# Gated attention and token MLP on one core: one transpose for the bias rows, and Wk loaded in two held halves

## The chip, the cores and the metric

The kernel runs on one core of one Trainium2 chip. The metric is device time in microseconds (us) of one execution. TensorE is called PE here, VectorE DVE, ScalarE ACT, GpSimd POOL and SyncE SP, as the profile calls them. SP, ACT and POOL each issue DMA transfers from a queue of their own.

## The reference

The input `x` has 2048 rows of 512 numbers in bfloat16. The output mixes two branches with a gate per row:

```
g   = sigmoid((x * gate_w).sum(-1))
qkv = x @ wqkv                      # 512 x 1536; 32 heads of 16
a   = attention(q, k, v) @ wo       # each row sees 8 earlier rows, 2 apart, softmax over them
h   = layernorm(x)
u   = gelu(h.T @ w1 + b1)           # token MLP: 2048 -> 1792
b   = (u @ w2 + b2).T               # 1792 -> 2048
out = g * a + (1 - g) * b
```

`b1` has 1792 numbers, `b2` has 2048 and `gate_w` has 512. On the chip they are needed as columns, with 128 of them down the partitions: 14 columns for `b1`, 16 for `b2`, 4 for `gate_w`.

## The kernel before

The kernel is a list of operations, each with an engine, an estimated duration, the named results that it reads and writes, and a priority. A list scheduler at build time (`_Sched`) puts them into one fixed order per engine and works out the semaphore waits. All PE operations are chained, so PE runs them in the order in which they are written. On each of the DMA queues the loads of the beginning are chained in the same way.

The beginning, which the change is about, goes like this.

- POOL fills `ONES`, makes the identity `IDENT` from it (L458 to L461), and then issues three small loads: `gate_w` into `GWR` (4 rows of 128), `b1` into `B1R` (14 rows) and `b2` into `B2R` (16 rows) (L523 to L525). All three lie side by side in a region `ROWS`, each from partition 0 on. After that POOL writes padding and mask.
- SP and ACT issue the first loads in turn (L517 to L521): 128-row tiles 0 and 2 of `x` and quarters 0 and 2 of Wq on SP, tiles 1 and 3 and quarters 1 and 3 on ACT. Each has 128 KB. Then SP goes on alone, in this order: Wk as one load of 512 KB (L522), Wv (512 KB), and three times four tiles of `x` (512 KB) followed by a transposing load of the same rows into `XT`, and the first part of `w1`.
- PE starts with matmuls on constants that need no data (`f_warm`, L546). Then it transposes tiles 0 and 1 of `x` (`f_tx`, L562), DVE and ACT copy the results to `XT`, and PE multiplies with Wq, quarter by quarter of the contraction (`f_q0`, L583): `q0_0_0` and `q0_0_1`, with 256 columns. It transposes tiles 2 and 3, and does four more of these groups (16 matmuls of 256 columns).
- Next PE turns the bias rows into columns with three small transposes (`f_tb`, L599 to L601), into bank 7 of PSUM; DVE copies them out (L612 to L614). Then comes the last quarter of Wq over all 512 columns (`q0_2_3`).
- Then the projections run, 512 columns and four matmuls per PSUM bank each (`f_proj`, L650): K of the first 512 rows (four banks, "K block 0"), V of the first 512 rows (four banks), and then the rest, which reads the transposed loads. ACT empties the banks. A ring of seven banks is used in turn.

From there PE works through the projections (L650), the first layer of the MLP (L848), its second layer (L875) and the output product (L884). DVE does the attention in long element-wise operations (L449) beside it. PE takes their sums at L707 and L712 and their result at L884.

Of the kernel before, what the change touches and what calls it, by code (L numbers as in the profile page):

```python
# [5 lines left out]
BF16 = mybir.dt.bfloat16  # L6
# [7 lines left out]
D = 512  # L14
# [4 lines left out]
NST = S // 128  # L19
NFT = F // 128  # L20
# [260 lines left out]
class _Mem:  # L281
# [17 lines left out]
    def view(self, name, dtype, dims, extra=0, p0=0, np_=128):  # L299
        base = self.arena[:].bitcast(dtype)  # L300
        pst = base.ap[0][0]
        esz = mybir.dt.size(dtype)
        o = self.off[name]
        assert o % esz == 0
        return bass.AP(base.tensor, p0 * pst + o // esz + extra, [[pst, np_]] + [list(d) for d in dims])


def bass_gated_mix__sliding_local_dilated__mixer_token_mlp__prompt_kernel(nc, A_x, A_wqkv, A_wo, B_x, B_w1, B_b1, B_w2, B_b2, gate_w, out, dbg=None):
    with contextlib.ExitStack() as es:
        block = es.enter_context(nc.Block())  # L310
        m = _Mem(nc, es)
# [23 lines left out]
        m.region("OUTS", 5 * D * 2)  # L335
        m.region("RP", 32 * 2)
        m.region("GWREP", 4 * 32 * 2)
        m.region("ROWS", 384 * 2)
        m.region("MASK", NW * PAD * 2)
        m.region("SMALL", 2048)  # L340
        m.alias("UT", "WQKV")
# [4 lines left out]
        view = m.view  # L346
# [3 lines left out]
        A = sch.add  # L350
# [3 lines left out]
        wqkv_v = A_wqkv.rearrange("(dt p) c -> p dt c", p=128)  # L354
# [7 lines left out]
        WQKV = view("WQKV", BF16, [(3 * D, 4), (1, 3 * D)])  # L362
# [37 lines left out]
        IDENT = view("IDENT", BF16, [(1, 128)])  # L400
        ONES = view("ONES", BF16, [(1, 128)])
        RP = view("RP", BF16, [(1, 32)])
        GWREP = view("GWREP", BF16, [(32, 4), (1, 32)])
        MASK = view("MASK", BF16, [(PAD, NW), (1, PAD)], np_=32)
        B1R = view("ROWS", BF16, [(1, 128)], np_=NFT)
        B2R = view("ROWS", BF16, [(1, 128)], extra=128, np_=NST)
        GWR = view("ROWS", BF16, [(1, 128)], extra=256, np_=4)
        so = [0]

        def small(n, dims=None, extra=0):  # L410
# [21 lines left out]
        B2C = small(NST)  # L432
# [5 lines left out]
        def psb(bank):  # L438
            return ps[:, bank, :].bitcast(BF16)

        def sub(ap_, offs, dims):
            return bass.AP(ap_.tensor, ap_.offset + offs, [list(ap_.ap[0])] + [list(d) for d in dims])
# [12 lines left out]
        GELU = "gelu_apprx_tanh_and_others"  # L455
# [6 lines left out]
        A("pool", lambda e: e.memset(sub(KH[0], 0, [(KR, 4), (1, PAD)]), 0.0), 0.2, writes=["kpad"], name="kpad")  # L462
        A("pool", lambda e: e.memset(sub(V5, 0, [(VR, 4), (1, PAD)]), 0.0), 0.2, writes=["vpad"], name="vpad")

        def f_mask(e):
            ins = None
            for w in range(NW):
                if w:
                    ins = e.memset(psub(MASK, 0, 32, w * PAD, [(1, 2 * w)]), NEG)
                if 2 * w < PAD:  # L470
                    ins = e.memset(psub(MASK, 0, 32, w * PAD + 2 * w, [(1, PAD - 2 * w)]), 0.0)
            return ins
# [12 lines left out]
        def load(name, dst, src, nbytes, writes, transpose=False, queue="sp", issue=0.5, order=True, deps=(), after=()):  # L485
            ds = sch.dsem(name)

            def fn(e):
                if transpose:
                    return e.dma_start_transpose(dst, src)  # L490
                return e.dma_start(dst, src)  # L491
            op = sch.dma(queue, fn, nbytes, ds, issue=issue, writes=writes, deps=list(deps) + late_dep[0],
                         after=list(after) + ([last_ld[queue]] if order and queue in last_ld else []), name=name)
            if order:
                last_ld[queue] = op
            return op
# [14 lines left out]
        def xq(t, queue):  # L511
            return ld_first("x%d" % t, X[:, t:t + 1, :], xv[:, t:t + 1, :], 131072, ["x%d" % t], queue)

        def wqq(k_, queue):
            return ld_first("wq%d" % k_, WQKV[:, k_:k_ + 1, 0:D], wqkv_v[:, k_:k_ + 1, 0:D], 131072, ["wq%d" % k_], queue)

        for k_ in (0, 2):  # L517
            xq(k_, "sp")
            xq(k_ + 1, "act")
            wqq(k_, "sp")  # L520
            wqq(k_ + 1, "act")  # L521
        load("wk", WQKV[:, 0:4, D:2 * D], wqkv_v[:, 0:4, D:2 * D], 4 * 128 * D * 2, ["wk"])  # L522
        load("gw", GWR, gate_w.rearrange("(t p) -> t p", p=128), 1024, ["gwr"], issue=0.6, queue="pool")  # L523
        load("b1", B1R, B_b1.rearrange("(t p) -> t p", p=128), 4096, ["b1r"], issue=0.6, queue="pool")
        load("b2", B2R, B_b2.rearrange("(t p) -> t p", p=128), 4096, ["b2r"], issue=0.6, queue="pool")  # L525
        ld_w("wv", 2, 0, 4, "wv")
        for k_ in range(1, 4):
            ld_x(4 * k_, 4)
# [22 lines left out]
        def PE(fn, dur, reads, writes, name, prio=0):  # L551
            op = A("pe", fn, dur, reads=reads, writes=writes, after=([chain[0]] if chain[0] is not None else []), name=name, prio=prio)
            chain[0] = op
            return op
# [41 lines left out]
               "q0_%d_%d" % (hb, dt))  # L596

        def f_tb(e):
            e.transpose(out=psb(7)[:, 512:512 + NFT], in_=B1R, identity=IDENT[0:NFT, 0:NFT])  # L599
            e.transpose(out=psb(7)[:, 576:580], in_=GWR, identity=IDENT[0:4, 0:4])  # L600
            return e.transpose(out=psb(7)[:, 544:544 + NST], in_=B2R, identity=IDENT[0:NST, 0:NST])  # L601

        pe_tx(0)
        pe_q0(0, 0)
# [3 lines left out]
        pe_q0(1, 0)  # L608
        pe_q0(1, 1)
        pe_q0(1, 2)  # L610
        PE(f_tb, 0.17, ["b1r", "b2r", "gwr", "ident"], ["b7"], "t_b12")
        A("dve", lambda e: e.tensor_copy(out=GWREP, in_=sub(psb(7), 576, [(1, 4), (0, 32)])), 0.2, reads=["b7"], writes=["gwrep"], name="gwrep", prio=-20)  # L612
        A("dve", lambda e: e.tensor_copy(out=B1C, in_=psb(7)[:, 512:512 + NFT]), 0.15, reads=["b7"], writes=["b1c"], name="b1c", prio=-20)
        A("dve", lambda e: e.tensor_copy(out=B2C, in_=psb(7)[:, 544:544 + NST]), 0.15, reads=["b7"], writes=["b2c"], name="b2c", prio=-20)  # L614
        pe_q0(2, 3)
        XT0 = ["xt0_%d_%d" % (t, k_) for t in range(4) for k_ in range(2)]

# [3 lines left out]
        def evac(tn, dl, sb, bank, eng="act"):  # L621
            h, o = sb // 2, (sb % 2) * 512
            if tn == 0:
                dst = QH[h][:, dl, o:o + 512]
                A(eng, act(dst, ps[:, bank, :], AF.Copy, scale=0.25) if eng == "act" else
                  (lambda e: e.tensor_scalar(out=dst, in0=ps[:, bank, :], scalar1=0.25, scalar2=None, op0=ALU.mult)), 0.6,
                  reads=["b%d" % bank], writes=["q%d_%d" % (dl, sb)], name="evq%d_%d" % (dl, sb), prio=0 if eng == "act" else -25)
            elif tn == 1:
                dst = KH[h][:, dl, PAD + o:PAD + o + 512]
                A("act", act(dst, ps[:, bank, :], AF.Copy), 0.6, reads=["b%d" % bank], writes=["k%d_%d" % (dl, sb)],  # L630
                  name="evk%d_%d" % (dl, sb))
            else:
                dst = V5[:, dl, PAD + sb * 512:PAD + (sb + 1) * 512]
                A("act", act(dst, ps[:, bank, :], AF.Copy), 0.6, reads=["b%d" % bank], writes=["v%d_%d" % (dl, sb)],
                  name="evv%d_%d" % (dl, sb))
# [5 lines left out]
        def bank_():  # L641
            b = ring[1][ring[0] % len(ring[1])]
            ring[0] += 1
            return b

        def f_proj(tn, dl, sb, bank):
            def fn(e):
                ins = None
                for dt in range(4):
                    ins = e.matmul(ps[:, bank, :], lhsT=sub(WQKV, dt * 3 * D + tn * D + dl, [(4, 128)]),  # L650
                                   rhs=XT[:, dt, sb * 512:(sb + 1) * 512], start=(dt == 0), stop=(dt == 3))
                return ins
            return fn

        WR = {0: ["wq0", "wq1", "wq2", "wq3"], 1: ["wk"], 2: ["wv"]}

        def proj(tn, dl, sb):
            bank = bank_()
            PE(f_proj(tn, dl, sb, bank), 0.87, xt_res(sb) + WR[tn], ["b%d" % bank], "pj%s%d_%d" % ("qkv"[tn], dl, sb))
            evac(tn, dl, sb, bank)  # L660

        for dl in range(4):
            proj(1, dl, 0)
        for dl in range(4):
            proj(2, dl, 0)
        for dl in range(4):
# [3 lines left out]
          reads=["k%d_1" % dl for dl in range(4)], writes=["khalo"], name="khalo")  # L670
# [10 lines left out]
        for t in range(NST):  # L681
            A("dve", (lambda t_: lambda e: e.bn_stats(out=ST6[:, t_, :], in_=X[:, t_, :]))(t), 0.67,  # L682
              reads=["x%d" % t], writes=["st%d" % t], name="st%d" % t, prio=-20, after=[extl["dve"]])
# [6 lines left out]
          reads=["md"], writes=["vv"], name="ln_var", prio=-20)  # L690
# [3 lines left out]
          reads=["ms", "rstd"], writes=["nmr"], name="ln_nmr", prio=-20)  # L694
# [159 lines left out]
        for ft in range(NFT):  # L854
            bank = MLPB[ft]
            for half in range(2):
                PE(f_ph2(ft, bank, half), 1.735, ["x%d" % t for t in range(8 * half, 8 * half + 8)] + [W1R[ft // 2]], ["b%d" % bank],
                   "ph2_%d_%d" % (ft, half))
            A("act", act(UT[:, ft, :], ps[:, bank, :], AF.Gelu_apprx_tanh, bias=col(B1C, ft)), 0.7,
              reads=["b%d" % bank, "b1c"], writes=["ut%d" % ft] + (["wq0", "wq1", "wq2", "wq3", "wk", "wv"] if ft == 0 else []), name="gel%d" % ft, table=GELU)  # L860
            if ft % 2 == 1 and ft // 2 + 5 <= 6:
                ld_w1(ft // 2 + 5)
        for j in range(8):
# [40 lines left out]
        for i, half in head + tuple((i, half) for i in range(3, L) for half in range(2)):  # L904
            bank = banks[i]
# [103 lines left out]
```

## Time and profile before

| | |
|---|---|
| median of 5 runs | 166.07 us (165.59 to 166.25) |
| the profiled execution | 167.1 us, of which 165.4 us are the span from the first to the last instruction |
| granted PE clock over the span | 1.000 |
| PE | busy 160.4 us, 97% of the span |
| DVE | busy 150.8 us, 91% |
| ACT | busy 75.5 us, 46% |
| POOL | busy 13.7 us, 8% |

The profile is one execution. The timeline view gives the start and the duration of an instruction, or of a row of equal ones, from the span's start. Matmuls overlap in the pipeline: each is recorded for longer than the distance to the next, so the distance between starts is the time that one takes from PE. "Idle before" is the time that an engine waited, and what released it. For DMA, the view of issues gives the time from the start of the issue to the landing of the last byte. Rows marked SPq and ACTq are those queues' issue work.

### The profile page before, as it was taken

What the parts mean: (1) busy time and instruction counts of PE and PEld (TensorE: products, weight loads), DVE (VectorE), ACT (ScalarE), POOL (GpSimd) and SP (SyncE); (2) the same over time, 40 slices, a digit from 0 to 9 for tenths busy, and PEclk for the clock granted to TensorE, in tenths of its full rate; (3) what the DMA queues carried; (4) which work ended last, traced back from release to release, by engine and by line L of the source; (5) the groups of instructions that cost most, each with busy time, mean ns of one, the idle gap of its engine ahead of it and who ended that gap; (6) DMA issues with size and microseconds to landing.
All of it is one profiled execution on the core that took longest, in us unless ns stands there. A gap on an engine that the chain in (4) does not pass through costs nothing.

```text
span 165.4 us, 1993 instructions
## 1 busy us (share of the span) xinstructions
PE 160.4 (97%) x795; PEld 78.2 (47%) x810; DVE 150.8 (91%) x126; ACT 75.5 (46%) x104; POOL 13.7 (8%) x38
## 2 busy tenths in 40 slices
PE   7899999999999999999999999999999999999993
PEld 3665555555544444444444344444444444444551
DVE  0389999999999999999999999999999999999940
ACT  3327678667765399962221559310022111111164
POOL 7000110020000000005000000005000222000000
PEclk9999999999999999999999999999999999999999
DMA  5999989509399096999998983993995899981014
GB/s 141 300 289 270 226 187 256 115 15 190 63 292 317 26 244 180 298 290 285 168 220 231 271 244 101 302 271 108 284 231 170 163 207 189 210 187 35 32 54 137
DMA packets 44696, 32.24 MB, mean 195 GB/s; under 512 B 7952, under 2 KB 42256, under 8 KB 44688
## 3 DMA queue, kind: packets, MB, share of 16 engines
q1 hardware_dynamic: 41360, 22.06, 50.5%
q0 software_dynamic: 2608, 9.45, 28.3%
q10 hardware_dynamic: 720, 0.62, 1.1%
q8 instruction: 6, 0.10, 0.2%
q14 instruction: 2, 0.02, 0.0%
HBM read 18.88 MB, written 2.10 MB: 127 GB/s over the span
## 4 chain that ended last, share of the span: by engine, by line
PE 94%; DMA 2%; ACT 1%; issue 1%; SPq 0%
PE ps L848 29%; PE ps L875 29%; PE ps L650 23%; PE ps L884 8%; PE ps L583 3%; DMA arena<-in_A_wqkv_dram 2%; PE ps L712 1%; ACT arena L452 1%; PE ps L707 1%; PE ps L562 1%; SPq L491 0%; PE ps L599 0%; PE ps L601 0%; PE ps L600 0%
## 5 line engine op out<-in xcount | busy, mean ns | idle before, releaser
L449 DVE TENSOR_TENSOR arena<-arena 128x4096 bf16<-128x4096 bf16 (+8 forms) x79 | 132.1, 1719 | 1.4 <-ACT arena L452 0.3
L875 PE MATMUL ps<-arena 128*128 128x512 bf16 (+2 forms) x234 | 50.0, 366 | 0.2
L848 PE MATMUL ps<-arena 128*128 128x512 bf16 x218 | 48.5, 379 | 0.3
L452 ACT ACTIVATE arena<-ps,arena 128x512 bf16<-128x512 f32 (+1 forms) x30 | 21.8, 731 | 59.0 <-PE ps L884 41.0
L452 ACT ACTIVATE arena<-ps 128x512 bf16<-128x512 f32 (+3 forms) x53 | 33.1, 629 | 19.7 <-PE ps L650 10.6
L650 PE MATMUL ps<-arena 128*128 128x512 bf16 x173 | 38.0, 379 | 0.2
L875 PEld LDWEIGHTS ps<-arena 128*128 128x128 bf16 x238 | 22.8, 98 | 25.9
L848 PEld LDWEIGHTS ps<-arena 128*128 128x128 bf16 x224 | 21.7, 98 | 26.8 <-ACT arena L452 0.7
L650 PEld LDWEIGHTS ps<-arena 128*128 128x128 bf16 x176 | 19.9, 113 | 18.1
L884 PE MATMUL ps<-arena 128*128 128x512 bf16 (+2 forms) x67 | 15.6, 366 | 0.1
L944 ACT ACT_TABLE_LOAD x11 | 14.1, 1283 | 2.9 <-issue 2.7
L780 POOL DMA_DIRECT2D arena<-arena x8 | 4.4, 562 | 74.2 <-DVE arena L449 74.2
L884 PEld LDWEIGHTS ps<-arena 128*128 128x128 bf16 x68 | 6.5, 98 | 7.3
L682 DVE BATCH_NORM_STATS2 arena<-arena 128x6 f32<-128x512 bf16 x16 | 9.9, 678 | 0.0
L452 ACT ACTIVATE arena<-arena 128x16 f32<-128x16 f32 (+5 forms) x10 | 6.8, 679 | 6.2 <-DVE arena L449 6.0
L574 DVE COPY arena<-ps 128x256 bf16<-128x256 bf16 x4 | 1.2, 291 | 5.2 <-PE ps L562 4.9
L583 PE MATMUL ps<-arena 128*128 128x256 bf16 (+1 forms) x27 | 5.0, 348 | 0.7 <-DMA arena<-in_A_wqkv_dram 0.5
L696 DVE TENSOR_SCALAR arena<-arena 128x512 bf16<-128x512 bf16 x16 | 5.3, 407 | 0.0
L817 POOL DMA_DIRECT2D arena<-arena x3 | 3.6, 1200 | 19.0 <-DVE arena L449 19.0
L737 POOL DMA_DIRECT2D arena<-arena x2 | 2.5, 1234 | 30.0 <-DVE arena L449 30.0
L583 PEld LDWEIGHTS ps<-arena 128*128 128x128 bf16 x28 | 3.3, 128 | 1.7 <-DVE arena L574 0.8
L924 DVE TENSOR_SCALAR arena<-ps,arena 128x128 bf16<-128x128 f32 x1 | 0.4, 409 | 3.9 <-PE ps L884 3.9
(35 smaller groups left out, 19.8 us busy)
## 6 DMA issues: line engine op xcount, KB each, us to landing
arena<-in_B_w_dram SPq DMA_DIRECT2D x7, 1024.0 KB, 9.5
arena<-in_B_w_dram SPq DMA_DIRECT2D x8, 896.0 KB, 8.4
arena<-arena POOLq DMA_DIRECT2D x5, 1024.0 KB, 9.5
arena<-arena POOLq DMA_DIRECT2D x8, 512.0 KB, 11.0
out_dram<-arena SPq DMA_DIRECT2D x15, 128.0 KB, 1.7
arena<-in_A_x_dram SPq DMA_DIRECT2D x3, 512.0 KB, 4.8
arena<-in_A_wqkv_dram SPq DMA_DIRECT2D x2, 512.0 KB, 6.7
arena<-in_A_wo_dram SPq DMA_DIRECT2D x1, 512.0 KB, 8.8
```

The costliest lines, as they stand in the source:

```text
L449: return lambda e: e.tensor_tensor(out=o_, in0=a_, in1=b_, op=op_)
L452: return lambda e: e.activation(out=o_, in_=i_, func=f_, **kw)
L583: ins = e.matmul(ps[:, dl, c0:c1], lhsT=sub(WQKV, dt * 3 * D + dl, [(4, 128)]), rhs=XT[:, dt, c0:c1], start=(dt == 0 and hb == 0), stop=(d ...
L650: ins = e.matmul(ps[:, bank, :], lhsT=sub(WQKV, dt * 3 * D + tn * D + dl, [(4, 128)]), rhs=XT[:, dt, sb * 512:(sb + 1) * 512], start=(dt = ...
L682: A("dve", (lambda t_: lambda e: e.bn_stats(out=ST6[:, t_, :], in_=X[:, t_, :]))(t), 0.67, reads=["x%d" % t], writes=["st%d" % t], name="s ...
L696: A("dve", (lambda t_: lambda e: e.tensor_scalar(out=X[:, t_, :], in0=X[:, t_, :], scalar1=col(RSTD, t_), scalar2=col(NMR, t_), op0=ALU.mu ...
L780: prev = sch.dma("pool", (lambda d_, s_: lambda e: e.dma_start(d_, s_))(dst, src), 524288, sch.dsem("av%d_%d" % (h, c)), issue=1.0, reads= ...
L817: sch.dma("pool", (lambda o_, i_: lambda e: e.dma_start(o_, i_, accum_op=ALU.add, max_dma_last_dim=4096))(pw(0, 4), pw(4, 4)), 1800000, sc ...
L848: ins = e.matmul(ps[:, bank, :], lhsT=W1H[ft // 2][:, st, 128 * (ft % 2):128 * (ft % 2) + 128], rhs=X[:, st, :], start=(st == 0), stop=(st ...
L875: ins = e.matmul(ps[:, bank, 0:c1 - c0], lhsT=W2S[i // 2][:, ft, 128 * (i % 2):128 * (i % 2) + 128], rhs=UT[:, ft, c0:c1], start=(ft == 0) ...
L884: ins = e.matmul(ps[:, bank, 0:c1 - c0], lhsT=OT[:, i // 2, dl, 128 * (i % 2):128 * (i % 2) + 128], rhs=WO[:, dl, c0:c1], start=False, sto ...
L944: e.preload_act_table_set(want)
```

## The change

The three small loads go into one tile `ROWS` of 128 x 128, at partitions 0, 16 and 32. POOL writes zeros to all of the tile before. One 128 x 128 transpose replaces the three, and DVE picks the columns from other places. Wk is loaded in two halves of 256 KB (quarters 0 and 1 of the contraction, and 2 and 3). Both wait until tile 0 of `x` has landed; they stay at the same place of SP's queue, after the four first loads and ahead of Wv. The first two banks of K block 0 are filled in matching halves: two matmuls into the first bank, two into the second, then the other two of each. The other two banks go as before. A resource list at the first gelu names the two halves in place of the one load.

In the built programs the order of all other operations on every engine is the same in both. POOL has one memset more, ahead of that for `ONES`; SP has one issue more; PE has two matmuls less.

```diff
-        m.region("ROWS", 384 * 2)
+        m.region("ROWS", 128 * 2)
...
+        ROWS = view("ROWS", BF16, [(1, 128)])
         B1R = view("ROWS", BF16, [(1, 128)], np_=NFT)
-        B2R = view("ROWS", BF16, [(1, 128)], extra=128, np_=NST)
-        GWR = view("ROWS", BF16, [(1, 128)], extra=256, np_=4)
+        B2R = view("ROWS", BF16, [(1, 128)], p0=16, np_=NST)
+        GWR = view("ROWS", BF16, [(1, 128)], p0=32, np_=4)
...
+        rows0 = A("pool", lambda e: e.memset(ROWS, 0.0), 0.15, name="rows0", prio=-90)
...
+        xld = {}
         for k_ in (0, 2):
-            xq(k_, "sp")
+            xld[k_] = xq(k_, "sp")
...
-        load("wk", WQKV[:, 0:4, D:2 * D], wqkv_v[:, 0:4, D:2 * D], 4 * 128 * D * 2, ["wk"])
-        load("gw", GWR, ..., issue=0.6, queue="pool")
-        load("b1", B1R, ..., issue=0.6, queue="pool")
-        load("b2", B2R, ..., issue=0.6, queue="pool")
+        for k_ in range(2):
+            load("wk%d" % k_, WQKV[:, 2 * k_:2 * k_ + 2, D:2 * D], wqkv_v[:, 2 * k_:2 * k_ + 2, D:2 * D], 2 * 128 * D * 2, ["wk%d" % k_], deps=[xld[0]])
+        load("gw", GWR, ..., issue=0.6, queue="pool", deps=[rows0])
+        load("b1", B1R, ..., issue=0.6, queue="pool", deps=[rows0])
+        load("b2", B2R, ..., issue=0.6, queue="pool", deps=[rows0])
...
         def f_tb(e):
-            e.transpose(out=psb(7)[:, 512:512 + NFT], in_=B1R, identity=IDENT[0:NFT, 0:NFT])
-            e.transpose(out=psb(7)[:, 576:580], in_=GWR, identity=IDENT[0:4, 0:4])
-            return e.transpose(out=psb(7)[:, 544:544 + NST], in_=B2R, identity=IDENT[0:NST, 0:NST])
+            return e.transpose(out=psb(7)[:, 512:640], in_=ROWS, identity=IDENT)
...
-        PE(f_tb, 0.17, ["b1r", "b2r", "gwr", "ident"], ["b7"], "t_b12")
+        PE(f_tb, 0.06, ["b1r", "b2r", "gwr", "ident"], ["b7"], "t_b12")
...
-        for dl in range(4):
+        kb0 = [bank_() for dl in range(2)]
+        for k_ in range(2):
+            for dl in range(2):
+                PE(f_proj(1, dl, 0, kb0[dl], 2 * k_, 2 * k_ + 2), 0.44, XT0 + ["wk%d" % k_], ["b%d" % kb0[dl]], "pjk%d_0_%d" % (dl, k_))
+                if k_ == 1:
+                    evac(1, dl, 0, kb0[dl])
+        for dl in range(2, 4):
             proj(1, dl, 0)
```

More of the change, by code (lines that the diff above doesn't have):

```diff
@@ L521, in bass_gated_mix__sliding_local_dilated__mixer_token_mlp__prompt_kernel @@
             wqq(k_ + 1, "act")
-        load("wk", WQKV[:, 0:4, D:2 * D], wqkv_v[:, 0:4, D:2 * D], 4 * 128 * D * 2, ["wk"])
-        load("gw", GWR, gate_w.rearrange("(t p) -> t p", p=128), 1024, ["gwr"], issue=0.6, queue="pool")
-        load("b1", B1R, B_b1.rearrange("(t p) -> t p", p=128), 4096, ["b1r"], issue=0.6, queue="pool")
-        load("b2", B2R, B_b2.rearrange("(t p) -> t p", p=128), 4096, ["b2r"], issue=0.6, queue="pool")
+        for k_ in range(2):
+            load("wk%d" % k_, WQKV[:, 2 * k_:2 * k_ + 2, D:2 * D], wqkv_v[:, 2 * k_:2 * k_ + 2, D:2 * D], 2 * 128 * D * 2, ["wk%d" % k_], deps=[xld[0]])
+        load("gw", GWR, gate_w.rearrange("(t p) -> t p", p=128), 1024, ["gwr"], issue=0.6, queue="pool", deps=[rows0])
+        load("b1", B1R, B_b1.rearrange("(t p) -> t p", p=128), 4096, ["b1r"], issue=0.6, queue="pool", deps=[rows0])
+        load("b2", B2R, B_b2.rearrange("(t p) -> t p", p=128), 4096, ["b2r"], issue=0.6, queue="pool", deps=[rows0])
         ld_w("wv", 2, 0, 4, "wv")
@@ L610, in bass_gated_mix__sliding_local_dilated__mixer_token_mlp__prompt_kernel @@
         pe_q0(1, 2)
-        PE(f_tb, 0.17, ["b1r", "b2r", "gwr", "ident"], ["b7"], "t_b12")
-        A("dve", lambda e: e.tensor_copy(out=GWREP, in_=sub(psb(7), 576, [(1, 4), (0, 32)])), 0.2, reads=["b7"], writes=["gwrep"], name="gwrep", prio=-20)
+        PE(f_tb, 0.06, ["b1r", "b2r", "gwr", "ident"], ["b7"], "t_b12")
+        A("dve", lambda e: e.tensor_copy(out=GWREP, in_=sub(psb(7), 544, [(1, 4), (0, 32)])), 0.2, reads=["b7"], writes=["gwrep"], name="gwrep", prio=-20)
         A("dve", lambda e: e.tensor_copy(out=B1C, in_=psb(7)[:, 512:512 + NFT]), 0.15, reads=["b7"], writes=["b1c"], name="b1c", prio=-20)
-        A("dve", lambda e: e.tensor_copy(out=B2C, in_=psb(7)[:, 544:544 + NST]), 0.15, reads=["b7"], writes=["b2c"], name="b2c", prio=-20)
+        A("dve", lambda e: e.tensor_copy(out=B2C, in_=psb(7)[:, 528:528 + NST]), 0.15, reads=["b7"], writes=["b2c"], name="b2c", prio=-20)
         pe_q0(2, 3)
@@ L644, in bank_, with f_proj @@
             return b
-        def f_proj(tn, dl, sb, bank):
+        def f_proj(tn, dl, sb, bank, d0=0, d1=4):
             def fn(e):
                 ins = None
-                for dt in range(4):
+                for dt in range(d0, d1):
                     ins = e.matmul(ps[:, bank, :], lhsT=sub(WQKV, dt * 3 * D + tn * D + dl, [(4, 128)]),
@@ L653, in f_proj @@
             return fn
-        WR = {0: ["wq0", "wq1", "wq2", "wq3"], 1: ["wk"], 2: ["wv"]}
+        WR = {0: ["wq0", "wq1", "wq2", "wq3"], 1: ["wk0", "wk1"], 2: ["wv"]}
         def proj(tn, dl, sb):
@@ L859, in bass_gated_mix__sliding_local_dilated__mixer_token_mlp__prompt_kernel @@
             A("act", act(UT[:, ft, :], ps[:, bank, :], AF.Gelu_apprx_tanh, bias=col(B1C, ft)), 0.7,
-              reads=["b%d" % bank, "b1c"], writes=["ut%d" % ft] + (["wq0", "wq1", "wq2", "wq3", "wk", "wv"] if ft == 0 else []), name="gel%d" % ft, table=GELU)
+              reads=["b%d" % bank, "b1c"], writes=["ut%d" % ft] + (["wq0", "wq1", "wq2", "wq3", "wk0", "wk1", "wv"] if ft == 0 else []), name="gel%d" % ft, table=GELU)
             if ft % 2 == 1 and ft // 2 + 5 <= 6:
```

## The prediction

> **What bounds the kernel now.** I read the engine shares first, then the chain that ended last, then the timeline of the beginning, where all edits lie.
>
> From the page, engine shares and chain of waits:
>
> ```profile
> PE 160.4 (97%) x795; PEld 78.2 (47%) x810; DVE 150.8 (91%) x126; ACT 75.5 (46%) x104; POOL 13.7 (8%) x38
> PE 94%; DMA 2%; ACT 1%; issue 1%; SPq 0%
> ```
>
> PE is the bound, and 94% of the chain is PE's own work. The 2% of DMA is one piece at the start (from 1.27, 3.81 us: Wq's first quarter). So time comes only from PE slots that vanish or from PE's early idle time. It then reaches the end if nothing downstream is later than PE.
>
> The timeline of PE in the first 12 us (start, duration):
>
> ```profile
> 0.85 2.72 PE L546 MATMUL ps<-const-bfloat16-1.0 128*128 128x512 bf16 x9 [0.85 <-PEq L994]
> 3.63 1.01 PE L562 MATMUL ps<-arena 128*128 128x128 bf16 x8
> 5.17 1.87 PE L583 MATMUL ps<-arena 128*128 128x256 bf16 x8 [0.53 <-DMA arena<-in_A_wqkv_dram]
> 6.83 1.06 PE L562 MATMUL ps<-arena 128*128 128x128 bf16 x8
> 7.69 2.35 PE L583 MATMUL ps<-arena 128*128 128x256 bf16 x16
> 9.97 0.18 PE L599 MATMUL ps<-arena 14*128 14x14 bf16 x1
> 10.01 0.16 PE L600 MATMUL ps<-arena 4*128 4x4 bf16 x1
> 10.04 0.16 PE L601 MATMUL ps<-arena 16*128 16x16 bf16 x1
> 10.38 0.81 PE L583 MATMUL ps<-arena 128*128 128x512 bf16 x3 [0.17 <-issue]
> ```
>
> Three things are to be seen. PE waits 0.53 for Wq's first quarter. From 5.17 on it never stops, but runs slowly at first: eight matmuls of 256 columns take 1.66 (5.17 to 6.83), 0.21 each; the last five of the sixteen before the bias transposes stand 0.11 apart. (All sixteen take 2.19; 0.11 each would be 1.75, so about four were slow, and the fast rate began near 8.6, some 3.4 after 5.17.) And three tiny transposes hold PE from 9.88 (last matmul's start 9.77 plus 0.11) to 10.38: 0.50 us.
>
> DMA view of the first 5 us (busy tenths in 40 slices of 0.125; issues, the last column us to landing):
>
> ```profile
> DMA  0000000000000019746899888999998758689999
> ...
> arena<-in_A_wqkv_dram SPq DMA_DIRECT2D x2, 512.0 KB, 6.7
> arena<-in_A_x_dram SPq DMA_DIRECT2D x2, 128.0 KB, 3.7
> arena<-in_A_x_dram ACTq DMA_DIRECT2D x2, 128.0 KB, 3.9
> arena<-in_A_wqkv_dram SPq DMA_DIRECT2D x2, 128.0 KB, 4.3
> arena<-in_B_b_dram POOLq DMA_DIRECT2D x1, 4.0 KB, 5.4
> ```
>
> Asked one issue at a time, the same view gives the landings: x tile 0 at 3.5, Wq's quarters 0 and 1 at 5.1 and 5.3, x tiles 2 and 3 at 6.4 and 6.7, Wq's quarters 2 and 3 at 7.0 and 7.2, Wk 8.9, Wv 10.3, b2 8.1. PE needs Wk at 11.02, so Wk is 2.1 early and its two halves can save nothing there by themselves.
>
> **The change part by part.**
>
> *Three transposes become one.* Removed: 0.50 us of PE. Added: one matmul of 128 columns. Slow, such a one takes 0.11 (eight in 6.83 to 7.69); at the fast rate half of the 0.11 for 256 columns is 0.055. At full size, as the x transposes are, it passes into the next group without a gap (7.69 follows on the cadence). Between 0.055 and 0.11, and if the 0.10 idle ahead of L599 comes from its three semaphore waits and stays, 0.16 to 0.21: the saving lies between 0.29 and 0.445. I take 0.43: entering the narrow matmuls at L707 costs the same extra (three L848 matmuls from 53.55 at 0.216 end at 54.19, L707 starts at 54.28: 0.09), without data being late, so the gap goes with the narrow shape.
>
> *POOL's memset* costs 0.20 (the 128 x 128 memset of `ONES`) and pushes identity and small loads by that at most. The identity is ready by 1.4 and used at 3.63; b2 lands at 8.3 in place of 8.1 and is needed at 9.9. Cover 1.6, cost nothing; uncovered it would be 0.2. The DVE copies are the same three.
>
> *The hold.* SP would issue Wk at 2.68; now it stands until x tile 0 is in (3.5). Behind it on SP are the second half, Wv, x tiles 4 to 7, the transposing loads and `w1`. One more issue costs 0.43 (a Wq issue on SP), so all of these are issued up to 0.9 + 0.43 = 1.3 later. Who waits for that: K block 0 at about 10.6 (Wk lands at 8.9; 10.2 if fully shifted), V at 14.5 (10.3, 11.6), bn_stats of tile 4 at 15.04 (11.7, 13.0), the first transposed load at 17.9 (13.5, 14.8), bn_stats of tile 12 at 22.0 (20.3, 21.6). All keep cover; the least is some 0.4. Uncovered, the price is at most 1.3 minus the cover.
>
> What can the hold gain? Less traffic beside the eight first loads could bring in Wq's first quarter sooner than 5.1. PE can't start before ACT's copy of tile 1 ends (timeline of ACT: 4.25 plus 0.81, of which the first copy ends at 4.64), so at most 0.4; and x tile 2 lands at 6.4 against a start at 6.83, which leaves 0.37 until that load moves too. Bounds: 0.37 gained, or, if the loads spread by the same amount the other way, 0.37 lost. I take 0.1 gained, nearer to zero than to the end: Wq's first quarter has been issued at 1.27, Wk in the old order at 2.68, and an issue takes 1.0 to reach the data (first issue 0.82; the strip shows first bytes near 1.8), so Wk could disturb only the last 1.4 of the 3.8 that this load takes.
>
> [...]
>
> *K block 0 in halves.* The same eight matmuls at 0.216 in the two first banks: no PE time. The first bank is full after six matmuls in place of four, 0.43 later in the block. ACT is then 0.13 earlier than before (it was held at 12.19 by Q's copies), and DVE's first long product (12.83) starts about 0.13 earlier, not 0.43. DVE is thus 0.3 later against PE. Where PE takes DVE's results it has more cover than that: sums at 54.28 against 53 (DVE's third of four products after 48.47 ends at 52.95), last output product at 160.9 against 158.9.
>
> The sum: 0.43 + 0.10 = 0.53. The profiled execution takes 167.1, of which the span is 165.4 and 1.7 lies around it; it becomes 166.6. The median of the runs is 1.0 lower, 166.07, and becomes 165.5. About 0.3%, or 0.5 us, can be told from no change in this kernel, so the forecast lies just over that line.
>
> **The rivals.**
>
> *Only the transposes pay.* The loads land as before: 0.29 to 0.445 saved, 165.6 to 165.8. For it: the eight first loads stand ahead of Wk in either order. It falls inside 0.3%.
>
> *The loads gain fully.* 0.43 + 0.37 = 0.8, 165.3. It needs x tiles 2 and 3 to come sooner too. This ends on the forecast's side.
>
> *PE's fast rate comes later (slower).* PE reached the fast rate about 3.4 us after its last pause ended at 5.17; the constants and transposes from 0.85 on did not bring it. If Wq's first quarter comes at 4.7 and x tiles 2 and 3 still at 6.4 to 6.7, PE pauses inside that stretch. The count may start anew there: then up to 3.4 us more run at half speed, which loses 1.7. Less the 0.43 it makes 167.3; with half of that stretch, 166.5. The point from which it decides is a start before 5.17 minus (6.83 − 6.45) = 4.8, with the x tiles unmoved. Against it: the 0.06 between constants and transposes shows that PE can pause, but none of these rows shows what length of pause counts.
>
> [...]
>
> [...]
>
> **How the numbers follow.** Transposes plus some or all of the loads, 165.0 to 165.55: 0.51. Transposes alone, or with a small loss at the loads, 165.6 to 166.5: 0.30. Slower by the fast rate or a later first load, 166.6 to 167.3: 0.19. Faster by over 0.3% 0.51, within 0.3% 0.30, slower 0.19. The range reaches from both gains (165.3 less 0.4, most of the 0.48 by which the lowest run shown stands under their median: 164.9) into the slower case with half a stretch (166.5, and 0.2 for the spread: 166.7). The forecast case's own range is 164.9 to 165.6.
>
> **What would show it.** In the changed profile one matmul of 128 columns stands between the two L583 rows, no more than 0.2 of PE goes there, and the last L583 group starts 0.43 or more before 10.38. Wk's halves are issued after 3.5 and land before 11; PE idles nowhere in K block 0. The idle time before the first L583 row is 0.2 to 0.53, and the x tiles' transposes follow without a pause. Wrong would make it: a pause inside 5 to 8.6 with 0.21 distances that last beyond 9; a wait on Wk or on transposed loads in the L650 rows; or 0.3 or more left at the one transpose.

## The result: slower, by a load whose landing was held up

Over all runs the kernel before takes 165.95 us (median of 71, 165.36 to 167.95) and the changed kernel 167.64 (median of 36, 165.55 to 170.22). The ratio is 1.0044 with an interval of 1.0026 to 1.0063: slower by a little more than can be told from no change. Every ratio in this document leaves out runs more than 1.5% above a kernel's fastest, here 13 of the 36 with the profiled one among them, and since that profile shows the loss explained below, the ratio understates it: the medians stand 1.7 apart. More telling is how the times are spread: 27 of the 36 runs lie above 166.5, but only 10 of the 71 of before.

The profiled execution takes 169.73 us, of which the span is 168.0. From its page: engine shares, the granted PE clock in 40 slices of 4.2 us, the chain that ended last.

```profile
PE 160.2 (95%) x793; PEld 77.1 (46%) x808; DVE 150.8 (90%) x126; ACT 75.5 (45%) x104; POOL 13.8 (8%) x39
...
PEclk9999997899999999999999999999999999999999
...
PE 82%; SPq 8%; DMA 7%; ACT 1%; issue 1%
```

PE does the same 160 us of work, but it is 82% of the chain instead of 94%. SP's queue and a transfer have taken 15% of it, and the clock shows a dip around 28 us (each digit is the granted clock of a slice in tenths). The beginning, where I had looked for the whole effect, is not at fault. PE's timeline of the changed kernel (start, duration):

```profile
3.69 0.61 PE L567 MATMUL ps<-arena 128*128 128x128 bf16 x8
4.64 1.04 PE L588 MATMUL ps<-arena 128*128 128x256 bf16 x8 [0.34 <-DVE arena L579]
5.51 0.61 PE L567 MATMUL ps<-arena 128*128 128x128 bf16 x8
6.02 1.94 PE L588 MATMUL ps<-arena 128*128 128x256 bf16 x16
7.79 0.22 PE L604 MATMUL ps<-arena 128*128 128x128 bf16 x1
8.07 0.81 PE L588 MATMUL ps<-arena 128*128 128x512 bf16 x3
8.71 9.66 PE L653 MATMUL ps<-arena 128*128 128x512 bf16 x44
```

K block 0 starts at 8.71, which was 11.02 before: 2.3 sooner. The one transpose passes with hardly a gap (the row behind it has three matmuls on record of the four in the program; more on that below). So the time was lost later. The timeline from 14 to 36 us, with ACT, DVE, weight loads, the other loads and POOL's second transfer left out:

```profile
17.13 4.32 SPq L493 DMA_TRANSPOSE arena<-in_A_x_dram  x1
...
18.01 1.28 POOL L746 DMA_DIRECT2D arena<-arena  x1 [13.96 <-DVE arena L450]
...
26.66 9.62 PE L653 MATMUL ps<-arena 128*128 128x512 bf16 x35 [3.10 <-DMA arena<-in_A_x_dram]
```

SP issues the last transposing load (rows 1536 to 2047 of `x`) at 17.13. Only 0.88 later, POOL issues its first transfer of 1 MB that adds one SBUF tile to another (the operation `qd0_0`, L737 before, L746 now). PE starts its last matmul at 23.17 and runs dry, and starts again at 26.66, released by that load. How long the load took, from the DMA views of before (16 to 21 us) and after (17 to 22), the last column being us from issue to landing:

```profile
arena<-in_A_x_dram SPq DMA_TRANSPOSE x1, 6.0
```

```profile
arena<-in_A_x_dram SPq DMA_TRANSPOSE x1, 9.4
```

Its data were not late. The last of its 256-byte packets stands at 22.58 in the trace, 5.45 after the issue (5.39 before), but the landing is at 26.52. In between the DMA engines worked on the accumulating transfer. From the DMA view of the changed kernel, 22 to 27 us: queue, packets, MB, share of the 16 engines.

```profile
q0 software_dynamic: 240, 0.98, 98.3%
```

That is POOL's queue. The kernel before has 18.4% there in the same window. PE then goes on at half speed. From the table by stretch of the changed kernel (window and its length; busy time with counts of PE, weight loads, DVE, ACT and POOL; then PE's granted clock, DMA share, GB/s):

```profile
22.00:28.00 6.00, 2.90 (x14) 1.26 (x12) 5.89 (x15) 2.60 (x7) 0.00 (x0) 0.96 1.09 228
28.00:32.00 4.00, 4.00 (x13) 1.53 (x12) 4.00 (x13) 1.52 (x4) 0.00 (x0) 0.63 0.83 218
```

The trace's clock record has half rate from 27.55 to 30.97, 3.41 us, which loses 1.7. Wait and half rate together: from K block 0's start to the first layer of the MLP it takes 42.94 instead of 37.99. So 4.95 is lost after 2.31 was gained, which is the 2.6 by which the span grew.

### The profile page after: what moved, and what is told of

Same layout as the page of the kernel before. It is cut to its first block, busy times and chain, and to the rows that moved or that the text cites. A ratio compares the mean times of both kernels' runs of the same rounds, so it can differ in the third digit from the quotient of the medians.

```text
span 168.0 us, 1991 instructions
## 1 busy us (share of the span) xinstructions
PE 160.2 (95%) x793; PEld 77.1 (46%) x808; DVE 150.8 (90%) x126; ACT 75.5 (45%) x104; POOL 13.8 (8%) x39
## 4 chain that ended last, share of the span: by engine, by line
PE 82%; SPq 8%; DMA 7%; ACT 1%; issue 1%
PE ps L857 29%; PE ps L884 29%; PE ps L653 15%; PE ps L893 8%; DMA arena<-in_A_x_dram 7%; SPq L493 6%; SPq L494 2%; PE ps L721 1%; ACT arena L453 1%; PE ps L716 1%
## 5 line engine op out<-in xcount | busy, mean ns | idle before, releaser
L857 PE MATMUL ps<-arena 128*128 128x512 bf16 x218 | 48.5, 379 | 0.3
L653 PE MATMUL ps<-arena 128*128 128x512 bf16 x173 | 39.8, 391 | 3.3 <-DMA arena<-in_A_x_dram 3.1
L884 PEld LDWEIGHTS ps<-arena 128*128 128x128 bf16 x238 | 22.8, 98 | 25.9
L857 PEld LDWEIGHTS ps<-arena 128*128 128x128 bf16 x224 | 21.7, 98 | 26.9 <-ACT arena L453 0.7
L653 PEld LDWEIGHTS ps<-arena 128*128 128x128 bf16 x176 | 20.1, 115 | 22.8 <-issue 5.8
L893 PEld LDWEIGHTS ps<-arena 128*128 128x128 bf16 x68 | 6.5, 98 | 7.3
L746 POOL DMA_DIRECT2D arena<-arena x2 | 2.5, 1234 | 29.4 <-DVE arena L450 29.4
L588 PE MATMUL ps<-arena 128*128 128x256 bf16 (+1 forms) x27 | 3.8, 285 | 0.4 <-DVE arena L579 0.3
L551 PE MATMUL ps<-const-bfloat16-1.0 128*128 128x512 bf16 (+1 forms) x9 | 2.7, 484 | 0.8 <-PEq L1003 0.8
```

The source lines that it names most:

```text
L588: ins = e.matmul(ps[:, dl, c0:c1], lhsT=sub(WQKV, dt * 3 * D + dl, [(4, 128)]), rhs=XT[:, dt, c0:c1], start=(dt == 0 and hb == 0), stop=(d ...
L857: ins = e.matmul(ps[:, bank, :], lhsT=W1H[ft // 2][:, st, 128 * (ft % 2):128 * (ft % 2) + 128], rhs=X[:, st, :], start=(st == 0), stop=(st ...
L884: ins = e.matmul(ps[:, bank, 0:c1 - c0], lhsT=W2S[i // 2][:, ft, 128 * (i % 2):128 * (i % 2) + 128], rhs=UT[:, ft, c0:c1], start=(ft == 0) ...
L893: ins = e.matmul(ps[:, bank, 0:c1 - c0], lhsT=OT[:, i // 2, dl, 128 * (i % 2):128 * (i % 2) + 128], rhs=WO[:, dl, c0:c1], start=False, sto ...
```

## The experiments

My theory after the result, called the crossing: the earlier K block 0 starts, the sooner DVE reaches the product after which POOL issues `qd0_0`. If that comes too soon behind SP's issue of the last transposing load, the load's landing is held up and PE starves. The rivals were that the hold on Wk makes the transposed loads late as such, and that the loss comes with the new start of PE itself. "The guard" below is one added dependence: `qd0_0` also waits until the last transposing load has landed.

### The changed kernel with the guard

```diff
-            ld_xt(k_)
+            xtl = ld_xt(k_)
...
+                                     deps=[xtl] if (h, s_) == (0, 0) else [])     # operation qd0_0
```

> The changed kernel, with one wait more: POOL's first accumulating transfer (L746 of the changed kernel) starts only when the last transposed x load has landed. Theory A (crossing): the loss comes from that load's completion being held up behind the accumulating transfer, which the earlier start of PE and DVE has moved ahead to 18.0. Then the load lands by 22.7 in place of 26.5, PE's 3.5 us wait and the 3.4 us of half speed after it (5.0 us together) are gone, and the time is 164.0 to 165.8 by the start of the fast rate, faster than before by 0.2 to 1.2%. Rival B (the hold): the transposed loads are late because SP issues everything 1.1 us later; then PE still waits on x by 1 us or more and the time stays near 167.5. [...]

Measured: 165.63, ratio 0.9956 (0.9935 to 0.9978), none of 12 runs above 166.04. From the timeline, 14 to 36 us, filtered as above:

```profile
13.64 22.61 PE L653 MATMUL ps<-arena 128*128 128x512 bf16 x102
...
16.22 3.93 SPq L493 DMA_TRANSPOSE arena<-in_A_x_dram  x1
...
22.79 1.28 POOL L746 DMA_DIRECT2D arena<-arena  x1 [18.74 <-DVE arena L691]
```

PE's row runs through without a pause, the load landed at 22.19, and POOL issues afterwards. The whole change is still in; only the order of two transfers has been fixed. The loss is gone. (The view puts POOL's wait down to DVE, but in all seven guarded profiles POOL starts 0.61 after the load's landing, here 22.79 after 22.19.) The time, 165.63, is close to the forecast's 165.5, but this does not yet show the forecast gain: the guard alone also makes the kernel before faster, as shown below.

### Each part alone

The transposes alone (before with the zeroed tile and the one transpose; the scheduler's estimate for the memset was lowered so that its orders stay those of before):

```diff
+        rows0 = A("pool", lambda e: e.memset(ROWS, 0.0), 0.02, name="rows0", prio=-90)
...
-            e.transpose(out=psb(7)[:, 512:512 + NFT], in_=B1R, identity=IDENT[0:NFT, 0:NFT])
-            e.transpose(out=psb(7)[:, 576:580], in_=GWR, identity=IDENT[0:4, 0:4])
-            return e.transpose(out=psb(7)[:, 544:544 + NST], in_=B2R, identity=IDENT[0:NST, 0:NST])
+            return e.transpose(out=psb(7)[:, 512:640], in_=ROWS, identity=IDENT)
```

> The kernel before, with one change alone: the zeroed tile and the one 128 x 128 transpose; all orders as before. Theory A: PE saves what the two timelines show, 0.61 less 0.38 from the last narrow group's start to the next group, some 0.2 to 0.3; the x loads stay early, nothing crosses, 165.7. Rival B: the same, 165.7. Rival C: an earlier PE start shifts the fast rate; 165.5 to 168, with a wide spread.

Measured: 166.63, ratio 1.0031 (0.9997 to 1.0066). The 12 runs fall into two groups, six from 165.86 to 166.26 and six from 167.0 to 167.93. The profile fell in the upper one. Its timeline, 14 to 36 us:

```profile
16.54 3.92 SPq L493 DMA_TRANSPOSE arena<-in_A_x_dram  x1
...
18.48 1.28 POOL L739 DMA_DIRECT2D arena<-arena  x1 [14.42 <-DVE arena L450]
...
26.07 10.09 PE L652 MATMUL ps<-arena 128*128 128x512 bf16 x45 [1.74 <-DMA arena<-in_A_x_dram]
```

I had expected that nothing would cross here. But the crossing is there with no hold in the kernel: POOL 1.94 behind SP, data done at 21.95, landing at 25.94. PE's clock stayed at full rate after this wait of 2.1. So an execution without the hold can lose by this route. That the transposes make it more frequent is not shown: the interval takes in no change, and 11 of the 35 runs of before measured beside these lie above 166.5 too.

The hold alone (before, Wk still one load):

```diff
-        load("wk", WQKV[:, 0:4, D:2 * D], wqkv_v[:, 0:4, D:2 * D], 4 * 128 * D * 2, ["wk"])
+        load("wk", WQKV[:, 0:4, D:2 * D], wqkv_v[:, 0:4, D:2 * D], 4 * 128 * D * 2, ["wk"], deps=[xld[0]])
```

> The kernel before, with the hold alone: Wk as one load that waits for x tile 0. Theory A: if the hold makes the first loads land sooner (as in the changed kernel: Wq's first quarter 4.1, x tile 3 5.4), PE starts near 4.6, and the accumulating transfer crosses the last transposed load in part of the executions: 166 to 168. If the first loads land as before, DVE is as late as before, the accumulating transfer starts at 20 and the load ends by 23: 166.0. Rival B: the transposed loads are late whatever DVE does: 167 or more, with a wait on x in the L650 rows. Rival C: no effect of the hold but the lottery, 166.

Measured: 166.15, ratio 0.9996 (0.9966 to 1.0025). Four of 12 runs lie above 166.5, up to 168.33. The profile shows POOL 2.65 behind SP, a landing 1.3 after the data (22.04, 23.34) and no wait of PE. What made the four runs long was not profiled.

The change without the hold:

```diff
-            load("wk%d" % k_, WQKV[:, 2 * k_:2 * k_ + 2, D:2 * D], wqkv_v[:, 2 * k_:2 * k_ + 2, D:2 * D], 2 * 128 * D * 2, ["wk%d" % k_], deps=[xld[0]])
+            load("wk%d" % k_, WQKV[:, 2 * k_:2 * k_ + 2, D:2 * D], wqkv_v[:, 2 * k_:2 * k_ + 2, D:2 * D], 2 * 128 * D * 2, ["wk%d" % k_])
```

> The changed kernel without the hold: Wk's halves are issued at once after the first four loads. Theory A: the x loads are issued 0.4 later than before in place of 1.1, so that the last transposed load ends by 22.0 and the transfer that starts at 18 to 20 crosses it less often: 165.2 to 166.5. Rival B: no wait on x at all, 165.5. Rival C: as the changed kernel, 167 to 168.

Measured: 165.58, ratio 0.9967 (0.9948 to 0.9985), all 12 runs between 165.12 and 165.82. In the profile SP issues at 15.71 and POOL 3.24 later; data done 21.12, landed 21.64. Without the hold the change stays clear of the crossing: none of these 12 runs is long, against 27 of 36 with it.

### The same kernels, all with the guard

If the crossing explains the differences, they should vanish under the guard, except for what each part truly saves.

> The kernel before, with the guard alone: its first accumulating transfer (L737) waits until the last transposed x load has landed. Theory A (crossing): before, the accumulating transfer is issued near 19 to 20 and crosses that load only in some executions (those with PE and DVE early), so the guard takes away the upper tail and 0 to 0.3 us of the median: 165.7 to 166.0. Rival D: the guard gains by itself what the guarded change gained (0.4%), and transposes and halves bring nothing: 165.5 or less.

> The one 128 x 128 transpose alone, with the guard. Theory A: the loss of the transpose alone (ratio 1.003) was the crossing; with the guard the 0.23 us that all traces show between the last narrow group and the next (0.61 to 0.38) come out: 0.2 to 0.3 under the guarded kernel before, about 165.5, and no wait of PE on x in the L650 rows. Rival C: the start of the fast rate decides; no ordering against the guarded kernel before.

> One transpose and Wk's halves without the hold, with the guard. Theory A: the halves bring nothing on PE; 165.5, as with the transpose alone, and if the hold is worth nothing at the first loads it also equals the guarded change (165.6). Rival E (halves): loads and K block in halves bring 0.2 or more beyond the transpose: 165.3 or less.

> The hold alone (Wk in one load that waits for x tile 0), with the guard. Theory A: without crossings the hold is seen for what it does to the first loads: the same as the guarded kernel before within 0.2 us, 165.7 to 166.0; all later loads still land before PE needs them. Rival B: the hold costs by itself through later x loads: PE waits on x in the L650 rows, 166.3 or more.

Each ratio is taken to the runs of before measured beside that kernel. Their median was 166.34 in the second and third column and 166.00 in the last.

| kernel | median with the guard | ratio to before, with the guard | ratio to before, without the guard |
|---|---|---|---|
| before | 165.85 | 0.9970 (0.9949 to 0.9991) | 1 |
| transposes alone | 165.50 | 0.9955 (0.9932 to 0.9977) | 1.0031 (0.9997 to 1.0066) |
| change without the hold | 165.87 | 0.9960 (0.9932 to 0.9988) | 0.9967 (0.9948 to 0.9985) |
| hold alone | 166.08 | 0.9992 (0.9971 to 1.0014) | 0.9996 (0.9966 to 1.0025) |

The transposes alone go from the slowest of these four to the lowest median. Before itself gains 0.3% from the guard: 17 of the 35 runs measured beside it lie above 166.5, and under the guard none of its 12 lies above 166.38. That the long runs of before are crossings is therefore likely, but none of them was profiled with one: its profile of 167.1 has none, and was long because PE reached K block 0 late, at 11.02. The hold alone gains nothing with the guard either. By the guarded medians it is 0.2 worse than before, less than these intervals can separate. The change without the hold missed its expectation of 165.5: with 165.87 it is no faster than guarded before, though it has the one transpose.

The PE timelines of guarded before, and then of the guarded transposes, give the transposes' true price, as here all matmuls are on record:

```profile
6.69 1.98 PE L583 MATMUL ps<-arena 128*128 128x256 bf16 x16
8.60 0.18 PE L599 MATMUL ps<-arena 14*128 14x14 bf16 x1
8.64 0.16 PE L600 MATMUL ps<-arena 4*128 4x4 bf16 x1
8.66 0.17 PE L601 MATMUL ps<-arena 16*128 16x16 bf16 x1
8.76 1.05 PE L583 MATMUL ps<-arena 128*128 128x512 bf16 x4
```

```profile
6.54 1.94 PE L587 MATMUL ps<-arena 128*128 128x256 bf16 x16
8.32 0.22 PE L603 MATMUL ps<-arena 128*128 128x128 bf16 x1
8.38 1.03 PE L587 MATMUL ps<-arena 128*128 128x512 bf16 x4
```

From the start of the first of the transposes to that of the next group it takes 0.16 (8.60 to 8.76) against 0.06 (8.32 to 8.38). From the last 256-column matmul (8.395 in the trace of the first) to the first narrow transpose it takes 0.205, and 0.109 with the wide one. The sum of both differences, with a first step of 0.24 instead of 0.22 after the narrow ones, is some 0.23. The medians, 165.85 and 165.50, stand 0.35 apart, which fits, but their intervals overlap, and the guarded change without the hold does not show the gain.

### Late loads by themselves

To separate the lateness of the loads from the hold on Wk, the load of `x` tiles 4 to 7, which stands before the transposing loads on SP, was held in the kernel before. First until Wq's quarter 1 was in, without and with the guard:

```diff
+            wql[k_ + 1] = wqq(k_ + 1, "act")
...
+            ld_x(4 * k_, 4, [wql[1]] if k_ == 1 else [])
```

> The kernel before, with the load of x tiles 4 to 7 (and so every later load of SP) held until Wq's quarter 1 has landed: the x loads are issued about 1 us later, as in the changed kernel, and nothing else is touched. Theory A (crossing): the accumulating transfer's data starts at 21 to 22 in most executions, the last transposed load's data then ends at 22.3 to 23, the two cross, and the time is 166.5 to 168, with PE waiting 1 to 3 us on x in the L650 rows. Rival F (order, not lateness): only the whole change makes them cross; 166.0.

> The same late x loads, with the guard. Theory A: lateness of 1 us by itself is covered (PE needs the last transposed load near 24.3); 165.7 to 166.1, as the guarded kernel before. Rival B (the lateness itself costs): 166.5 or more, with PE waiting on x though nothing crosses.

Measured: 165.96 (0.9986, 0.9965 to 1.0007) and 165.90 (0.9988, 0.9964 to 1.0013). My expectation of 166.5 to 168 without the guard was missed, and the pair told nothing apart. That load was issued 0.6 later, but the last transposing load was issued at 15.95, no later than in before, and POOL came 2.76 behind it. The delay had been swallowed on the way, by SP's long issue of the first transposing load, which the last section shows. So the same load was held longer, until Wk was in:

```diff
+            xl = ld_x(4 * k_, 4)
...
+        x4l.deps.add(wkl)      # x tiles 4 to 7 wait for Wk; order of the queue unchanged
```

> The kernel before, with the load of x tiles 4 to 7 (and so every later load of SP) held until Wk has landed: the x loads are then issued 1 to 1.5 us later than before, the last transposing load near 17.3 in place of 16.0, while POOL's accumulating transfer is issued at 18.5 to 20 as before. Theory A (crossing): POOL's issue follows SP's by 1.2 to 2.7 us in place of 2.8 to 3.9; as in the changed kernel's first profile (0.9) and the transpose alone (1.9) the load lands 3 to 4 us after its data, PE waits 1 to 3 us, and the time is 167 to 168.5. Rival H (the hold on Wk itself is the cause): 166.0, no wait of PE.

> The same later x loads, with the guard. Theory A: lateness of 1 to 1.5 us is covered, the last transposed load lands near 23.5 against a need at 24.3; 165.7 to 166.3. Rival B (lateness itself): 166.8 or more, with a wait on x in the L650 rows.

Measured without the guard: 168.31, ratio 1.0091 (1.0057 to 1.0124), 10 of 11 runs above 166.5. With it: 165.86, ratio 0.9971 (0.9948 to 0.9994), the highest of 12 runs 166.17. The waits of the first, and its timeline of 14 to 36 us:

```profile
PE ps L652 <- DMA arena<-in_A_x_dram: 2.3, 1, 2.3
```

```profile
17.51 4.50 SPq L490 DMA_TRANSPOSE arena<-in_A_x_dram  x1
...
18.95 1.28 POOL L739 DMA_DIRECT2D arena<-arena  x1 [14.93 <-DVE arena L449]
...
27.10 9.15 PE L652 MATMUL ps<-arena 128*128 128x512 bf16 x34 [2.29 <-DMA arena<-in_A_x_dram]
```

And the timeline of the second:

```profile
13.73 22.61 PE L652 MATMUL ps<-arena 128*128 128x512 bf16 x104
...
16.87 3.91 SPq L490 DMA_TRANSPOSE arena<-in_A_x_dram  x1
...
23.42 1.28 POOL L739 DMA_DIRECT2D arena<-arena  x1 [19.39 <-DVE arena L684]
```

The first has POOL 1.44 behind SP, data done at 22.92, landing at 26.96, and after PE's wait 3.41 us at half rate: the changed kernel's picture, made in before by moving SP's issue later. In the second PE never pauses. So lateness of the loads costs nothing by itself, and the same lateness with POOL close behind does. The rival that lateness as such is the cause has fallen by this, and the one of PE's new start by the guarded change, which has the change's whole beginning and loses nothing.

### Both kernels once more

> The kernel before, unchanged, for a second profile. Theory A: the profile on which the prediction was built was a late one; in this one the fast rate starts near 4 to 6.5, PE enters the K block near 9.7 in place of 11.0, and the group after the narrow transposes has four matmuls, the first 0.1 after the last of them. Rival G: the first profile is typical, K block at 11.0 again.

> The changed kernel, unchanged, for a second profile. Theory A: where the accumulating transfer's data starts ahead of the end of the last transposed load's, that load lands 3 to 4 us after its last data and PE waits 1.5 to 3.5 us; where it starts after, the load lands at once and the span is 163.7 to 164.0. Rival C: the span follows the start of the fast rate and not the crossing.

Measured: 165.87 and 165.85, both with a span of 164.1. Here the changed kernel did not cross. Its timeline, 15 to 22 us:

```profile
15.79 3.89 SPq L493 DMA_TRANSPOSE arena<-in_A_x_dram  x1
19.07 1.28 POOL L746 DMA_DIRECT2D arena<-arena  x1 [15.00 <-DVE arena L450]
```

POOL is 3.28 behind SP, and the load landed 0.5 after its data. With 165.85 it belongs to the faster quarter of its runs. All nine profiles without the guard, by POOL's distance behind SP, which the landing follows in three steps (times from the traces, in us):

| profile | distance | landing after the last data | PE's wait |
|---|---|---|---|
| changed kernel | 0.88 | 3.9 | 3.5, then 3.4 at half rate |
| before, `x` held for Wk | 1.44 | 4.0 | 2.7, then 3.4 at half rate |
| transposes alone | 1.94 | 4.0 | 2.1 |
| hold alone | 2.65 | 1.3 | none |
| before again; `x` held for Wq | 2.76; 2.76 | 1.3; 1.3 | none |
| change without the hold | 3.24 | 0.5 | none |
| changed kernel again | 3.28 | 0.5 | none |
| before | 3.94 | 0.6 | none |

The wait is taken from the start of the last matmul ahead of it to that of the next. From K block 0's start to the end, the 13 profiles without a wait (these and the guarded ones) all take 154.33 to 154.37. The three with one take 156.24 (transposes alone), 158.45 (`x` held for Wk) and 159.29 (changed kernel). So nothing but this wait, with the half rate behind it, and the start of K block 0 sets these spans apart. In the seven guarded kernels 2 of 84 runs lie above 166.5, the higher at 166.77.

## Why the prediction was wrong

The forecast was 165.5 with 0.51 on faster. The kernel became slower.

**The step that failed is the hold's cover.** "All keep cover; the least is some 0.4" set the moved loads against the moment at which PE or DVE needs them. Its list has only the first of the three transposed loads; the last, for which PE then waited, is not in it. In before's profile that load landed at 22.07 and PE came to it at 25.70 (11.02 and 68 matmuls of 0.216), a cover of 3.6. Even in the changed profile it would have been in time with a quick landing: its data were there at 22.58, 0.5 to 0.6 more makes 23.2, and PE's next matmul was due at 23.39. The step did not ask what DVE's earlier work would release. DVE's second product ends sooner, POOL issues its accumulating transfer sooner, and by the runs above that transfer holds up this load's landing to 26.52. From before's profile to the changed one the distance shrank from 3.94 to 0.88: POOL came 2.0 earlier and SP 1.06 later. Against the second profile of before, with 2.76, they are 0.77 and 1.11. How the change makes this frequent is known in part only. The runs show that in the changed kernel it takes the hold (27 of 36 above 166.5 with it, none of 12 without). But SP's issue was as late as 17.13 in the first profile alone. In the other four with the hold it came at 15.79 to 16.65, much as without one (15.71 to 16.63, `x` held for Wk left out). "A wait on Wk or on transposed loads in the L650 rows" was named as a sign of being wrong, without a mechanism or a price.

**The rival that ended slower had the right consequence in the wrong place.** PE did lose 1.7 to half rate, but after the wait at 23 to 27 us and not at the start. By the runs, the wait comes first: the profile of the transposes alone loses 1.90 by it at full clock. That its price of 167.3 lies near the median of 167.64 is luck.

**The transposes' 0.43 was too large; it is 0.23.** It lies below the stated bounds of 0.29 to 0.445 too. The figure rested on "10.38 ... x3". There are four such matmuls, and the first was missing from the record, so one matmul's distance of 0.24 was booked as a gap. The narrow transposes hold PE not for 0.50 but for 0.26 (8.50 to 8.76 in guarded before). The count in the row said so.

**The profiled execution was not a typical one.** It was 1.0 above the median, and the prediction saw that, but priced the edits on its rows. In the second profile of before PE's fast rate begins at 3.82 instead of 8.58, and K block 0 at 9.80 instead of 11.02. In that of the changed kernel K block 0 starts at 9.77. So the 2.3 by which the first changed profile reached it sooner is mostly luck.

**The hold's 0.10 was not found.** `x` tile 2 landed at 5.2, 6.2, 6.4, 6.5 and 6.2 in profiles with the hold, and at 6.4, 6.0, 5.8, 5.9, 5.8, 5.9 and 6.0 without (the kernels with held `x` left out). Wq's first quarter landed at 3.9 to 4.1 with it and at 4.0 to 4.2 without, but for the 5.1 of the prediction's profile. For both loads the range with the hold overlaps the one without it, so no gain of 0.10 stands out from this spread.

**What held.** The load of `x` tiles 4 to 7 was issued 1.3 later, as forecast (5.02 against 3.71). POOL's memset stayed hidden: PE's first transposes start at 3.69 and 3.44 in the changed kernel, at 3.63 and 3.68 in before. The halves cost PE nothing: from K block 0's start to the MLP it takes 37.99 in twelve of the 13 profiles without a wait, and 38.02 in the guarded transposes alone. DVE came 0.3 later against PE, as forecast: POOL's first transfer is issued 8.98 after K block 0's start without the halves and 9.30 with them. That shift widens the distance. SP's issue also came sooner with the halves and no hold, at 15.71 and 15.75, against 15.95 to 16.63 in the seven profiles with Wk as one load and without a hold (the two with `x` held for Wk left out). So the halves help here by both ends, though no run has them alone.

## What to carry to other kernels

Before pricing an edit as "covered", follow what every engine that gets earlier will issue, and set it against the transfers that are in flight at that time; a cover in data is not a cover in completions (in the changed profile the data were there at 22.58 and PE was due at 23.39, but the landing came at 26.52). When the times of one kernel fall into groups, look for two events whose order is not fixed, and fix it with one dependence: the guard alone took 0.3% off the kernel before. The guard with the one transpose has the lowest ratio, 0.9955 (0.9932 to 0.9977), 165.50 against 166.34 measured beside it; the intervals of the guard alone and of the guarded change overlap it. And count the matmuls in a row before reading a gap from it.

## What the runs showed of the hardware

- A transposing load's completion came 3.9 to 4.0 us after its last data when an accumulating SBUF-to-SBUF transfer was issued from POOL 0.9 to 1.9 us behind it, 1.3 at 2.65 to 2.76, and 0.5 to 0.6 from 3.2 on. That the completion is held up is shown; what inside the queues does it is not. The accumulating packets began about 0.1 before the load's last data in a quick landing too (21.01 against 21.12, landed 21.64). What differs is how much of the accumulating transfer runs between the load's last data and its landing: 205 to 208 of its 256 packets of 4 KB in the three profiles with a wait, 65 in the three with 1.3, 17 at a distance of 3.24 and none in the others. In the three with a wait SP's whole queue stood still: it has no packet at all for 2.7 to 3.0 us after the load's last data (22.58 to 25.24 in the changed kernel).
- SP's issue of the first transposing load ended 1.1 to 1.2 after Wv's landing in fourteen profiles, wherever between 4.25 and 5.58 it began. It is the chain's longest piece on SP in the changed kernel:

```profile
5.58 6.94 SPq L493
```

  In the two profiles with `x` held for Wk, where it began at 9.01 and 9.26, it ended 1.9 and 2.0 after Wv. In all sixteen it ended 0.2 to 0.3 before the landing of `x` tiles 4 to 7, the load just ahead of it. So the landings ahead, and not the start of this issue, go with the start of the later loads; which of the two loads it follows is not shown. In the profiles of the halves with the hold Wv landed at 10.07, 10.30 and 11.32, without it at 9.73 and 10.10. Which cause made the 11.32 is open.
- Waits of PE of 2.7 and 3.5 us went with 3.41 us at half rate, from 27.06 (PE started again at 27.10) and from 27.55 (26.66); one of 2.1 did not. What sets the length of these stretches is not shown.
- PE's fast rate began between 3.5 and 8.6 us after the start, in executions of the same programs: 8.58 and 3.82 in before, 3.66 and 3.50 in the changed kernel.
